# Channel attention over a 384 x 384 x 384 image: eight packed blocks in place of seven, a halved second test step, and a second pass that opens in places of 18 rows

## The chip, the cores and the metric

One NeuronCore of a Trainium2 chip. The metric is the device time of one execution in microseconds, as the median of the runs given. x has 113 MB, the core's on-chip memory (SBUF) holds a quarter of it, so x must be read, for the most part, twice.

## The reference

```python
xf = x.reshape(B, H * W, C)                    # bfloat16, 147456 x 384
gap, gmp = jnp.mean(xf, 1), jnp.amax(xf, 1)    # sum and maximum of each channel
h_a = gap @ w1; h_a = h_a * (h_a > 0)
h_m = gmp @ w1; h_m = h_m * (h_m > 0)
scale = sigmoid(h_a @ w2 + h_m @ w2)
return x * scale[:, None, None, :]
```

A first pass over x makes one sum and one maximum for each of 384 channels; a tiny network turns them into 384 scales; a second pass multiplies x by them. The scales need the whole of x.

## The kernel before

**Rows.** x is cut into 1152 *rows*: a row here is 384 channels on each of 128 partitions, 128 x 768 B = 98,304 B. The tensor `rows` holds 280 *body* rows and 5 *held* rows; `acc` holds 11 more. What stays on chip from the first pass is only multiplied and written in the second; all else is read again.

**First pass** (the loop over `steps`; each load is issued at L373 on SyncE's queue SP). For each load, TensorE adds up the channels (`sums`, L276: a matmul with a vector of ones, three at a time for a group of up to four rows), VectorE takes maxima into `acc` (L342). Loads go round through the same body places: a load waits until VectorE, TensorE and, where a packed block is in the way, ScalarE have done with what lies there. Not more than eight transfers are under way, since each semaphore is used again by the eighth after it.

**Packed blocks.** Seven blocks of 32 rows are kept in 24 rows each: `homes` holds three parts of 8 rows, `fourth` the fourth part. ScalarE first tests the block (`test`): L303 squares a scaled high byte and stores a byte, L304 squares that byte less 4 and sums it up, five pairs for a block; a sum that isn't zero means that some value does not fit the packed form, and then the blocks are read again at the end. `pack(i, half)` does half a block: TensorE makes words out of the high bytes (L324, 24 matmuls into the PSUM tile `words`), ScalarE moves low bytes into the freed places (L330, two copies) and stores the words (L331). After that the place of the fourth part is free. `judge` (L337 to L339) adds the tests up; L555 and L556 read the verdict.

**Between the passes.** `turn_sums` (L286 and L287) turns the sums by copies on ScalarE and matmuls on TensorE, `tail_sums` (L292) takes the last four loads, and `turn_over` (L348) lays a block of eight rows aside in the PSUM tile of `words`. The weights are loaded (L402, L403), a block of eight rows is loaded into the place that `turn_over` freed (`refill`, L415), `acc` is folded to one row and its rows are loaded again (L413). L404 to L407 are the mean's half of the network, L426 to L431 the maximum's half, L432 and L433 make `scale_bc`.

**Second pass.** VectorE multiplies (L438), writes are issued from ScalarE's queue (L447, L453, L492), reads from SP's (L531). First come the rows that stayed: `OPENING`, acc, the held rows, the two blocks of eight, then the 96 rows of the ring. As each place of the ring is written, a block of x is read into it (`read`), in `PLACES` of 24 and later 30 rows; the ring is body rows 0 to 96, and 0 to 120 once packed block 1 is finished. One *turn* multiplies a place, issues its write and the next read, and then does that turn's `jobs`: `unpack(i, half)` (L470 and L475 on VectorE, six copies of L489 on ScalarE) or `finish(i)`, which multiplies the block's 24 + 8 rows. Blocks 0 and 1 are written by `finish(1)`, the others beside the last three turns (`after`).

Every engine works through its own list in program order, as written out by hand; a wait of one instruction holds up all that stand behind it on its engine or queue.

Of the kernel before, what the change touches and what calls it, by code (L numbers as in the profile page):

```python
# [8 lines left out]
ACT = mybir.ActivationFunctionType  # L9
# [4 lines left out]
F32 = mybir.dt.float32  # L14
# [15 lines left out]

RING = 96
G = 8
PACKED = 7

HOME_AT = (96, 184, 128, 152, 256, 232, 208)
D_AT = (120, 176)
BODY_ROWS = 280
FIRST_AT = (0, 104, 40, 64, 200, 176, 152)  # L40
FOURTH_AT = (24, 96, 32, 88, 128, 136, 144)

TOGETHER = (1, 2, 3)
SLOTS = ((0, 31), (31, 31), (62, 34))
SPARE = 93
PSUM_ROWS = 8
LATE_ROWS = 8
BANK_ROWS = 2
RING_BYTES = 256
HELD_ROWS = 5  # L50
# [26 lines left out]
FIRST_READ = (8, 16)  # L77
FILLS = 13
# [11 lines left out]
def kernel(  # L90
# [31 lines left out]
    def take(n):  # L122
        nonlocal at
        at += n
        return at - n, n
# [4 lines left out]
    late_block, kept_block, held_block = (take(sum(pieces)) for pieces in LAST_HELD)  # L130
    stay = [take(n) for _, n in SLOTS]
    refill = take(LATE_ROWS)
    passing_at, n_pass = at, TOT - at
    between = [[take(n) for _, n in group] for group in BETWEEN]
    passing = [take(n) for _, n in PASSING]
    last_passing = take(sum(LAST_PASSING[1]))
    assert at == TOT and sum(n for _, n in PLACES) == n_pass and held_block[1] == HELD_ROWS
    assert late_block[1] == LATE_ROWS and kept_block[1] == G and [sum(p) for p in STAYING] == [n for _, n in SLOTS]
    at = passing_at
# [27 lines left out]
    held, body = rows[:, 0:HELD_ROWS, :], rows[:, HELD_ROWS:HELD_ROWS + BODY_ROWS, :]  # L167
    slots = [body[:, lo:lo + n, :] for lo, n in SLOTS]
    spare = body[:, SPARE, :]
    homes = [body[:, lo:lo + 3 * G, :] for lo in HOME_AT]  # L170
    d_places = [body[:, lo:lo + G, :] for lo in D_AT]
    fourth = [d_places[i % 2] for i in range(PACKED)]
    tested = held[:, 0:G // 2, :].rearrange("p n c -> p (n c)").bitcast(U8)
    tests = held[:, G // 2, :].bitcast(F32)
    test_bias = tests[:, NT:NT + 1]
    minus4 = tests[:, NT + 1:NT + 2]
    test_sum = tests[:, NT + 2:NT + 3]
    test_copy = tests[:, NT + 3:2 * NT + 3]

# [28 lines left out]
    nc.vector.memset(test_bias, 4.5 * TEST_SCALE)  # L208
    nc.vector.memset(minus4, -4.0)
    make_identity(nc, ident_bf)  # L210
# [21 lines left out]
    def fill(block, lo):  # L232
        load(block, body[:, lo:lo + block[1], :], (block[1],))

    for i in range(PACKED):
        if i in TOGETHER:
            lo = min(HOME_AT[i], D_AT[i % 2])
            load(packed_block, body[:, lo:lo + GP, :], (GP,), min(FIRST_AT[i], FOURTH_AT[i]))
        else:
            load(packed_block, homes[i], (FIRST_LOAD, 3 * G - FIRST_LOAD) if i == 0 else (3 * G,), FIRST_AT[i])  # L240
            load(packed_block, fourth[i], (G,), FOURTH_AT[i])
        steps += [("test", i, 0), ("pack", i, 0), ("test", i, 1), ("test", i, 2)]
        if i == 0:
            fill(first_block, 0)
        for k, b in enumerate(between[i]):
            fill(b, BETWEEN[i][k][0])
            if k == PACK_BEHIND[i]:
                steps.append(("pack", i, 1))
    for k, b in enumerate(passing):
        fill(b, PASSING[k][0])  # L250
    fill(refill, REFILL_AT)
    load(last_passing, body[:, LAST_PASSING[0]:, :], LAST_PASSING[1])
    for k, pieces in enumerate(STAYING):
        load(stay[k], slots[k], pieces)
        if k == 0:
            steps.append(("judge",))
    for block, buf, pieces in zip((late_block, kept_block, held_block), (*d_places, held), LAST_HELD):
# [39 lines left out]
    def test_one(rows, k):  # L297

        run = rows.shape[1] if len(rows.shape) == 2 else rows.shape[1] * rows.shape[2]
        out_ = tested[:, 0:run]  # L300
        if len(rows.shape) == 3:
            out_ = out_.rearrange("p (r n) -> p r n", r=rows.shape[1])
        nc.scalar.activation(out=out_, in_=rows, func=ACT.Square, bias=test_bias, scale=TEST_SCALE)  # L303
        nc.scalar.activation(  # L304
            out=out_, in_=out_, func=ACT.Square, bias=minus4, accum_out=tests[:, k:k + 1],
        )
# [29 lines left out]
    def judge():  # L336
        nc.scalar.activation(out=test_copy, in_=tests[:, 0:NT], func=ACT.Copy, accum_out=test_sum)  # L337
        nc.scalar.copy(out=total, in_=test_sum)
        nc.tensor.matmul(bad_ps, lhsT=total, rhs=ones_bf, start=True, stop=True)  # L339

# [21 lines left out]
    for st in steps:  # L362
# [51 lines left out]

    nc.sync.dma_start(out=d_places[0], in_=rows_of(xr, refill))  # L415
    load_acc(folds[-1], A)
# [37 lines left out]


    turns = len(PLACES)
    homes_d = [d_places[i % 2] for i in range(4)]
    homes_d += [homes[1][:, G * i:G * (i + 1), :] for i in range(3)]
    assert len(homes_d) == PACKED
    HG = G // 2  # L460
# [36 lines left out]
    def finish(i):  # L497

        for rows in (homes[i], homes_d[i]):
            multiply(rows, rows)  # L500
        if i == 1:
            store_packed(HOME_AT[0], GP, 0)
            store_packed(D_AT[1], GP, FOURTH_AT[1])


    jobs = [[(unpack, 0, 0)], [(unpack, 0, 1)], [(unpack, 1, 0)], [(finish, 0)], [(unpack, 1, 1)], [], [(finish, 1)]]
    jobs += [[], [], [], [(unpack, 2, 0)], [(unpack, 2, 1)]]
    for i in range(3, PACKED):
        jobs += [[(unpack, i, 0)], [(finish, i - 1)], [(unpack, i, 1)]]
    jobs.append([])  # L510
    jobs.append([(finish, PACKED - 1)])

    after = [(D_AT[0], 2 * GP, FOURTH_AT[2]), (HOME_AT[5], 6 * G, FIRST_AT[5]), (HOME_AT[1], 6 * G, FOURTH_AT[4])]

# [21 lines left out]

    def put_slot(i, lo, pieces):
        put(stay[i], slots[i][:, lo:, :], pieces, lo)

    put_slot(*OPENING)  # L540
    put_acc()
    put(held_block, held, (HELD_ROWS,))
    put(kept_block, d_places[1], (G,))
    put(refill, d_places[0], (LATE_ROWS,))
    for pieces in FIRST_PLACE:
        put_slot(*pieces)
    read(-1, 0)
    for pieces in SECOND_PLACE:
        put_slot(*pieces)
    read(-1, 0)  # L550
    for pieces in OTHER_PLACES:
        put_slot(*pieces)
    read(-1, 0)
    read(-1, 0)
    nc.vector.tensor_scalar(out=flag, in0=bad_ps, scalar1=0.5, scalar2=None, op0=ALU.is_gt)  # L555
    bad = nc.values_load(flag, engines=(ENG.SP, ENG.Activation, ENG.DVE))  # L556
    assert len(jobs) <= turns - 3
    gone = 0
# [4 lines left out]
    for turn in range(turns):  # L563
        b, buf = order.pop(0)
        multiply(buf, buf)
        if turn >= turns - len(after):
            store_packed(*after[turn - turns])
        store(buf, b, 0)
        while read(turn, gone):
            pass  # L570
        for job, *which in jobs.pop(0) if jobs else ():
            job(*which)
            gone = gone or (job is finish and which[0] == 1)
        if turn == turns - 3:
            to = leaving[1][0]
            nc.vector.tensor_copy(out=to.bitcast(U32), in_=late.bitcast(U32))  # L576
            turn_over(late, to)
            multiply(leaving[0][0][:, 0:PSUM_ROWS, :], kept_ps)
            multiply(leaving[0][0][:, PSUM_ROWS:, :], kept_b)
            multiply(to, late)  # L580
    assert not again and not order and not jobs
    for to, block in leaving:
# [38 lines left out]
```

## Time and profile before

| | us |
|---|---|
| runs shown | 724.15, 724.43 (median), 724.96 |
| the profiled execution | 724.86 |
| its span, first to last instruction | 723.1 |
| VectorE busy | 563.9 (78%) |
| ScalarE busy | 349.8 (48%) |
| TensorE busy | 183.8 (25%) |
| DMA: 192.14 MB read, 113.25 MB written | mean 423 GB/s |
| the chain that ended last: DMA, VectorE | 63%, 28% of the span |

The first pass lasts to about 270 us, the second from about 275 us to the end. Busy time is a sum over stages: ScalarE, for one, is busy for over 95% of 20 to 240 us and idle for long stretches later. A row of the table of groups gives line, engine, operation, tiles and shape, the count, busy time, mean duration in ns, and what ended the engine's idle time ahead of these instructions.

### The profile page before, as it was taken

What the parts mean: (1) busy time and instruction counts of PE and PEld (TensorE: products, weight loads), DVE (VectorE), ACT (ScalarE), POOL (GpSimd) and SP (SyncE); (2) the same over time, 40 slices, a digit from 0 to 9 for tenths busy, and PEclk for the clock granted to TensorE, in tenths of its full rate; (3) what the DMA queues carried; (4) which work ended last, traced back from release to release, by engine and by line L of the source; (5) the groups of instructions that cost most, each with busy time, mean ns of one, the idle gap of its engine ahead of it and who ended that gap; (6) DMA issues with size and microseconds to landing.
All of it is one profiled execution on the core that took longest, in us unless ns stands there. A gap on an engine that the chain in (4) does not pass through costs nothing.

```text
span 723.1 us, 3872 instructions
## 1 busy us (share of the span) xinstructions
PE 183.8 (25%) x1354; PEld 73.1 (10%) x1354; DVE 563.9 (78%) x441; ACT 349.8 (48%) x251; POOL 0.7 (0%) x6
## 2 busy tenths in 40 slices
PE   5577475966777560000000000000000000001000
PEld 1222122322222140000000000000000000001000
DVE  5698999999999998797966454798888889496200
ACT  6999999997999200057230032806244451300000
POOL 0000000000000000000000000000000000000000
PEclk9888878896978555555555555555555555555555
DMA  9999999999999979999999999999999999999997
GB/s 381 431 441 436 420 435 429 432 426 433 430 427 425 424 314 385 396 433 429 432 432 429 436 426 432 424 435 433 430 435 436 430 432 430 435 435 431 441 426 341
DMA packets 21123, 305.63 MB, mean 423 GB/s; under 512 B 2704, under 2 KB 2928, under 8 KB 8176
## 3 DMA queue, kind: packets, MB, share of 16 engines
q1 hardware_dynamic: 13760, 192.14, 62.4%
q10 hardware_dynamic: 7344, 113.25, 36.7%
q8 instruction: 10, 0.16, 0.1%
q14 instruction: 9, 0.07, 0.0%
HBM read 192.14 MB, written 113.25 MB: 422 GB/s over the span
## 4 chain that ended last, share of the span: by engine, by line
DMA 63%; DVE 28%; issue 3%; SPq 0%; DVEq 0%
DMA rows<-in_x_dram 44%; DVE acc L342 19%; DMA out_dram<-rows 18%; DVE rows L438 8%; DMA acc<-in_x_dram 1%; DVE rows L470 1%; DVE acc L438 0%; SPq L373 0%; DVE acc L475 0%; DVE acc L470 0%; SPq L531 0%; DVEq L438 0%; DVEq L342 0%
## 5 line engine op out<-in xcount | busy, mean ns | idle before, releaser
L438 DVE TENSOR_TENSOR rows<-rows,scale_bc 128x9216 bf16<-128x9216 bf16 (+9 forms) x56 | 230.9, 4166 | 93.7 <-DMA rows<-in_x_dram 92.7
L342 DVE TENSOR_TENSOR acc<-acc,rows 128x2304 bf16<-128x2304 bf16 (+4 forms) x234 | 245.2, 1126 | 12.7 <-DMA rows<-in_x_dram 12.5
L489 ACT COPY rows<-rows 128x1536 uint8<-128x1536 uint8 x28 | 41.3, 1476 | 206.4 <-DVE rows L438 205.7
L276 PE MATMUL bank_a<-rows,small 128*1 128x512 bf16 (+3 forms) x888 | 94.8, 473 | 82.0 <-DMA rows<-in_x_dram 82.0
L348 PE MATMUL words_ps<-ident_bf,acc 128*128 128x128 bf16 x24 | 2.7, 313 | 378.4 <-DVE acc L576 378.4
L303 ACT ACTIVATE rows<-rows 128x3072 uint8<-128x3072 int8 (+1 forms) x35 | 81.9, 2341 | 10.5 <-DMA rows<-in_x_dram 9.8
L304 ACT ACTIVATE rows<-rows 128x3072 uint8<-128x3072 uint8 (+1 forms) x35 | 82.0, 2344 | 1.1
L489 ACT COPY rows<-acc 128x1536 uint8<-128x1536 uint8 x42 | 60.5, 1473 | 18.2 <-DVE acc L475 17.7
L276 PEld LDWEIGHTS <-small 128*1 128x1 bf16 x888 | 30.4, 95 | 142.9 <-issue 122.0
L348 PEld LDWEIGHTS <-acc 128*128 128x128 bf16 x24 | 2.5, 148 | 378.6 <-DVE acc L576 378.6
L330 ACT COPY rows<-rows 128x1536 uint8<-128x1536 uint8 x28 | 39.7, 1468 | 0.3 <-PE words_ps L324 0.3
L324 PE MATMUL words_ps<-rows,scale_bc 128*128 128x512 fp8e4 (+1 forms) x126 | 37.0, 405 | 9.0 <-ACT rows L331 9.0
L324 PE MATMUL words_ps<-rows 128*128 128x512 fp8e3 (+1 forms) x126 | 35.1, 388 | 0.0
L470 DVE TENSOR_SCALAR rows<-rows 128x1536 uint16<-128x1536 uint16 x56 | 31.3, 560 | 1.9
L324 PE MATMUL words_ps<-rows,w_sb 128*128 128x512 fp8e3 x84 | 26.4, 398 | 0.0
L489 ACT COPY acc<-rows 128x1536 uint8<-128x1536 uint8 x14 | 20.5, 1467 | 0.0
L331 ACT ACTIVATE rows<-words_ps 128x1536 uint16<-128x1536 f32 x14 | 20.1, 1438 | 0.0
L324 PEld LDWEIGHTS <-scale_bc 128*128 128x128 bf16 x126 | 12.0, 101 | 29.2 <-issue 17.7
L324 PEld LDWEIGHTS <-rows 128*128 128x128 bf16 x126 | 12.7, 101 | 16.2 <-issue 2.4
L475 DVE SCALAR_TENSOR_TENSOR rows<-rows 128x768 uint32<-128x768 uint32 x14 | 13.4, 959 | 0.5
L475 DVE SCALAR_TENSOR_TENSOR acc<-acc,rows 128x768 uint32<-128x768 uint32 x14 | 13.4, 958 | 0.5
L286 ACT COPY w_sb<-bank_a 65x128 f32<-65x128 f32 x2 | 0.5, 261 | 25.0 <-PE bank_a L276 24.4
(61 smaller groups left out, 70.4 us busy)
## 6 DMA issues: line engine op xcount, KB each, us to landing
rows<-in_x_dram SPq DMA_DIRECT2D x16, 2880.0 KB, 26.8
out_dram<-rows ACTq DMA_DIRECT2D x15, 2880.0 KB, 21.4
rows<-in_x_dram SPq DMA_DIRECT2D x15, 2304.0 KB, 18.5
out_dram<-rows ACTq DMA_DIRECT2D x14, 2304.0 KB, 21.1
rows<-in_x_dram SPq DMA_DIRECT2D x4, 3072.0 KB, 32.1
rows<-in_x_dram SPq DMA_DIRECT2D x14, 768.0 KB, 14.0
out_dram<-rows ACTq DMA_DIRECT2D x2, 4608.0 KB, 45.6
rows<-in_x_dram SPq DMA_DIRECT2D x4, 2016.0 KB, 25.7
```

The source lines that it names most:

```text
L276: nc.tensor.matmul(sum_ps[q * QP:q * QP + 1, 0:g * P], lhsT=ones_bf[:, 0:1], rhs=rows[:, k:k + g, q * P:(q + 1) * P], start=(done + k == 0 ...
L303: nc.scalar.activation(out=out_, in_=rows, func=ACT.Square, bias=test_bias, scale=TEST_SCALE)
L304: nc.scalar.activation(out=out_, in_=out_, func=ACT.Square, bias=minus4, accum_out=tests[:, k:k + 1],)
L324: nc.tensor.matmul(words[:, c:c + BANK], lhsT=weights[2 * r + k], rhs=high(part(i, r), dt)[:, half * n + c:half * n + c + BANK], start=(r ...
L330: nc.scalar.copy(out=high(part(i, r), U8)[:, span], in_=low(part(i, r + 2), U8)[:, span])
L331: nc.scalar.activation(out=part(i, 2).rearrange("p n c -> p (n c)").bitcast(U16)[:, span], in_=words, func=ACT.Copy, bias=32767.5,)
L342: nc.vector.tensor_tensor(out=out_, in0=in0, in1=in1, op=ALU.max)
L348: nc.tensor.transpose(out=out_[:, r, q * P:(q + 1) * P], in_=rows[:, r, q * P:(q + 1) * P], identity=ident_bf)
L438: nc.vector.tensor_tensor(out=dst, in0=src, in1=scale_bc.unsqueeze(1).to_broadcast([P, n, C]), op=ALU.mult)
L470: nc.vector.tensor_scalar(out=u16(dst), in0=u16(src), scalar1=s1, scalar2=s2, op0=op0, op1=op1)
L475: nc.vector.scalar_tensor_tensor(out=u32(v), in0=u32(v), scalar=0x3F3F3F3F, in1=u32(m), op0=ALU.bitwise_xor, op1=ALU.bitwise_xor)
L489: nc.scalar.copy(out=dst, in_=src)
```

## The change

- Eight packed blocks. The eighth is loaded behind the others' (`LAST_BLOCK`, 10 and 22 rows, into body rows 64 to 96) and tested and judged there; its two pack halves are put ahead of the 19th and the 11th load from the end (`PACK_LAST`), and `judged`, the matmul of the verdict, ahead of the second half. It stays in body rows 72 to 96; rows 64 to 72 get a second block of eight rows between the passes, by a DMA ahead of the weights' loads.
- The rows that stay are body rows 0 to 64, not 0 to 96, and the loads of the first pass that only pass through at its end use these 64 rows too.
- The second step of a test reads and writes its bytes as uint16 pairs: half the elements, and the square of the pair less 0x0404.
- The second pass: a ring of 72 rows in places of 18 for twelve turns, then of 24 four times, then of 30. The eighth block's first half is unpacked ahead of the first turn. Blocks 7, 0, 2 and 3 are written when finished (`LEAVE`), the others beside the last three turns (`AFTER`); `TURNS` lists each turn's jobs (`7b` unpacks the second half of block 7, `f7` finishes it).
- `tests` has a tile of its own; the DMA scratch is 128 B, not 256.

```diff
-RING = 96
+RING = 72
-PACKED = 7
+PACKED = 8
-HOME_AT = (96, 184, 128, 152, 256, 232, 208)
-D_AT = (120, 176)
+HOME_AT = (96, 184, 128, 152, 256, 232, 208, 72)
+D_AT = (120, 176, 120, 176, 120, 176, 120, 64)
+D_THEN_AT = (120, 144, 120, 176, 136, 128, 120, 176)
-SLOTS = ((0, 31), (31, 31), (62, 34))
+STAY_ROWS = 64
-RING_BYTES = 256
+RING_BYTES = 128
-PASSING = ((62, 21), (0, 15), (15, 12), (31, 16), (47, 14))
-REFILL_AT = 62
-LAST_PASSING = (70, (6, 11))
-STAYING = ((8, 12, 11), (8, 7, 8, 8), (10, 4, 8, 4, 8))
+LAST_BLOCK = (10, 22)
+PACK_LAST = {19: 0, 11: 1}
+PASSING = ((0, 20), (20, 16), (36, 17), (53, 11), (0, 11), (11, 8), (19, 8), (27, 12))
+REFILLS = (5, 6)
+STAYING = ((39, (4, 8, 5, 8)), (0, (8, 4, 9, 8, 6, 4)))
-    ((0, 24), (24, 24), (48, 24), (72, 24)) * 3 + ((96, 24),)
-    + ((0, 30), (30, 30), (60, 30), (90, 30)) * 3 + ((0, 30), (30, 30), (60, 30), (90, 20))
+    ((0, 18), (18, 18), (36, 18), (54, 18)) * 3 + ((0, 24), (24, 24), (48, 24), (72, 24))
+    + ((0, 30), (30, 30), (60, 30), (90, 30)) * 3 + ((0, 30), (30, 30), (60, 30), (90, 12))
-FIRST_READ = (8, 16)
+FIRST_READ = (6, 12)
-OPENING = (0, 24, (3, 4))
-FIRST_PLACE = ((0, 8, (8, 8)), (0, 0, (8,)))
-SECOND_PLACE = ((1, 0, (8, 9)), (2, 0, (10,)))
-OTHER_PLACES = ((1, 17, (14,)), (2, 10, (24,)))
+OPENING = (57, (3, 4))
+FIRST_PLACE = (0, (9, 9))
+SECOND_PLACE = (18, (9, 9))
+THIRD_PLACE = (36, (18,))
+FOURTH_PLACE = (54, (3,))
+EARLY = "7a"
+TURNS = (
+    "", "7b", "", "f7", "0a", "", "0b", "f0", "", "2a", "", "2b", "f2", "3a", "3b", "f3", "", "1a", "1b",
+    "f1 4a", "4b", "f4 5a", "5b", "f5 6a", "6b", "f6",
+)
+LEAVE = {7: ((72, 24, 8), (176, 8, 0)), 0: ((96, 32, 32),), 2: ((120, 32, 64),), 3: ((152, 32, 96),)}
+GROW = (7, 0)
+AFTER = ((120, 32, 128), (184, 48, 160), (232, 48, 208))
...
+    i = PACKED - 1
+    load(packed_block, body[:, D_AT[i]:, :], LAST_BLOCK, FOURTH_AT[i])
+    steps += [("test", i, 0), ("test", i, 1), ("test", i, 2), ("judge",)]
...
         out_ = tested[:, 0:run]
+        pairs = out_.bitcast(U16)
...
         nc.scalar.activation(
-            out=out_, in_=out_, func=ACT.Square, bias=minus4, accum_out=tests[:, k:k + 1],
+            out=pairs, in_=pairs, func=ACT.Square, bias=minus, accum_out=tests[:, k:k + 1],
         )
...
+    def judged():
         nc.tensor.matmul(bad_ps, lhsT=total, rhs=ones_bf, start=True, stop=True)
...
+        if len(loads) - nth in PACK_LAST:
+            half = PACK_LAST[len(loads) - nth]
+            if half == 1:
+                judged()
+            pack(PACKED - 1, half)
         nc.sync.dma_start(out=rows, in_=rows_of(xr, block)[:, lo:hi, :])
...
+    nc.sync.dma_start(out=fourth[PACKED - 1], in_=rows_of(xr, refills[1]))
     nc.sync.dma_start(out=w1_sb, in_=w1.rearrange("(q p) m -> p q m", p=P))
...
+    put(refills[1], fourth[PACKED - 1], (G,))
     read(-1, 0)
+    work(EARLY)
...
-        for job, *which in jobs.pop(0) if jobs else ():
-            job(*which)
-            gone = gone or (job is finish and which[0] == 1)
+        if turn < len(TURNS):
+            work(TURNS[turn])
+            gone += sum("f%d" % i in TURNS[turn].split() for i in GROW)
```

More of the change, by code (lines that the diff above doesn't have):

```diff
@@ L248 @@
                 steps.append(("pack", i, 1))
+    i = PACKED - 1
+    load(packed_block, body[:, D_AT[i]:, :], LAST_BLOCK, FOURTH_AT[i])
+    steps += [("test", i, 0), ("test", i, 1), ("test", i, 2), ("judge",)]
     for k, b in enumerate(passing):
         fill(b, PASSING[k][0])
[L251 to L256, printed above, removed]
+    for lo, pieces in STAYING:
+        load(stay, body[:, lo:, :], pieces, lo)
     for block, buf, pieces in zip((late_block, kept_block, held_block), (*d_places, held), LAST_HELD):
@@ L413, in load_acc @@
         nc.sync.dma_start(out=acc[:, lo:hi, :], in_=acc_rows(xr, lo, hi))
[L415 removed]
+    nc.sync.dma_start(out=d_places[0], in_=rows_of(xr, refills[0]))
     load_acc(folds[-1], A)
@@ L500, in finish, with work @@
             multiply(rows, rows)
[L501 to L513, printed above, removed]
+        for leaves in LEAVE.get(i, ()):
+            store_packed(*leaves)
+    def work(turn):
+        for job in turn.split():
+            if job[0] == "f":
+                finish(int(job[1]))
+            else:
+                unpack(int(job[0]), "ab".index(job[1]))
     order = []
@@ L565 @@
         multiply(buf, buf)
-        if turn >= turns - len(after):
-            store_packed(*after[turn - turns])
+        if turn >= turns - len(AFTER):
+            store_packed(*AFTER[turn - turns])
         store(buf, b, 0)
@@ L580 @@
             multiply(to, late)
-    assert not again and not order and not jobs
+    assert not again and not order
     for to, block in leaving:
```

61 lines of the change are left out of this document (27 added, 34 removed).

## The prediction, made before the changed kernel was run

> **What bounds the kernel now.** First the page's slices of time and its bytes: is anything full all the time?
>
> ```profile
> DMA  9999999999999979999999999999999999999997
> GB/s 381 431 441 436 420 435 429 432 426 433 430 427 425 424 314 385 396 433 429 432 432 429 436 426 432 424 435 433 430 435 436 430 432 430 435 435 431 441 426 341
> HBM read 192.14 MB, written 113.25 MB: 422 GB/s over the span
> ```
>
> The DMA engines are busy from end to end; each slice (18.1 us) moves about 430 GB/s, except the first, the last, and the three from 253 to 307 us, where the first pass turns into the second. So time is bytes over 430 GB/s plus what that gap wastes. A row of all partitions (128 x 768 B = 98,304 B) costs 0.2286 us. I cut the gap into windows of 4 us (columns: time, busy us and count of PE, PEld, DVE, ACT, POOL, granted clock, DMA share, GB/s):
>
> ```profile
> 260.00:264.00 4.00, 1.92 (x15) 0.40 (x14) 4.00 (x6) 0.00 (x0) 0.00 (x0) 0.50 1.01 417
> 264.00:268.00 4.00, 3.64 (x45) 3.04 (x39) 4.00 (x5) 0.95 (x4) 0.00 (x0) 0.50 0.64 243
> 268.00:272.00 4.00, 3.37 (x62) 3.24 (x60) 3.90 (x7) 0.34 (x2) 0.00 (x0) 0.67 0.33 73
> 272.00:276.00 4.00, 1.04 (x7) 0.51 (x7) 2.29 (x6) 0.49 (x1) 0.00 (x0) 0.76 0.97 362
> 276.00:280.00 4.00, 0.00 (x0) 0.00 (x0) 3.83 (x5) 0.00 (x0) 0.00 (x0) 0.50 0.94 367
> 280.00:284.00 4.00, 0.00 (x0) 0.00 (x0) 4.00 (x4) 0.00 (x0) 0.00 (x0) 0.50 0.98 403
> ```
>
> Against 430 the last five lack 187 + 357 + 68 + 63 + 27 = 702 GB/s, times 4 us / 430 = 6.5 us of idle DMA. What ends the gap stands in the timeline (start, duration):
>
> ```profile
> 240.00 0.19 ACT L338 CAST small<-rows 128x1 bf16<-128x1 f32 x1
> 264.64 0.26 ACT L286 COPY w_sb<-bank_a 65x128 f32<-65x128 f32 x1 [24.44 <-PE bank_a L276]
> 267.40 2.72 PE L348 MATMUL words_ps<-ident_bf,rows 128*128 128x128 bf16 x24
> 271.16 0.17 ACT L404 ACTIVATE small<-bank_b 128x3 bf16<-128x3 f32 x1 [4.89 <-PE bank_b L292]
> 272.33 0.28 PE L426 MATMUL bank_a<-ident_bf,acc 128*128 128x128 bf16 x2 [0.69 <-DVE acc L342]
> ```
>
> Two chains meet: VectorE's maxima end in L426 at 272.33; the sums on TensorE and ScalarE (L286, L404) are through 0.7 us earlier (PE idle 0.69 before L426). ScalarE, busy from 20 to 240 us, then waits 24.4 us for L286. That idle time is the room of the change. Last, the prices by shape:
>
> ```profile
> L304 ACT ACTIVATE rows<-rows 128x3072 uint8<-128x3072 uint8 x21 | 60.0, 2856 | 0.7
> L303 ACT ACTIVATE rows<-rows 128x3072 uint8<-128x3072 int8 x21 | 59.9, 2851 | 10.0 <-DMA rows<-in_x_dram 9.8
> L330 ACT COPY rows<-rows 128x1536 uint8<-128x1536 uint8 x28 | 39.7, 1468 | 0.3 <-PE words_ps L324 0.3
> L304 ACT ACTIVATE rows<-rows 128x1536 uint8<-128x1536 uint8 x14 | 22.1, 1575 | 0.5
> L331 ACT ACTIVATE rows<-words_ps 128x1536 uint16<-128x1536 f32 x14 | 20.1, 1438 | 0.0
> ```
>
> **The bytes.** None is saved: rows read twice are 782 + 8 + 11 before (second-pass places, refill, acc) and 774 + 8 + 8 + 11 now, 801 both times. Eight of them move from the second pass, which is full, to the new refill DMA behind the first pass, into the 6.5 us of idle DMA: 8 x 0.2286 = 1.83 us gained. The cover is that gap; without it the gain is 0.
>
> **The test's second step** (L304) now has half the elements. No row shows an ACTIVATE from and to uint16; bounds: no gain (2.856 us) and 1.44 (L331, which writes uint16). I take the row of the same operation and count, 1.575; for 768 elements 1.575 - 768 x (2.856 - 1.575)/1536 = 0.935. A block saves 3 x 1.281 + 2 x 0.640 = 5.12 us of ScalarE.
>
> **The eighth block on ScalarE**, the step on which most hangs, since its pack stands in program order ahead of L286's copies. Before, a block takes 32.2 us without waits (207.55 to 239.76 in the timeline); now 32.2 - 5.1 = 27.1. Block 5 starts at 175.43 as before (ScalarE waits for its load there) and ends near 202.9 with 0.4 us of waiting for TensorE's words. Block 6 can't start before its load lands (TensorE starts on it at 203.81): 203.85. Its first pack half waits some 1.4 us for TensorE, whose 24 products start only behind the sums of 32 rows: end at 203.85 + 27.1 + 1.4 = 232.3. Block 7's 32 rows land at about 224, so no wait: tests 27.1 - 2 x 4.1 = 18.9 to 251.1, judge 0.5, first pack half 4.1: 255.7. Only then is PSUM free for TensorE's last 24 products. The like case, block 6's second half after a wait of 2.8 us, took 220.82 to 228.84 = 8.0 us with a granted clock of 0.53, then 0.96; bounds 5.4 (178.76 to 184.1, all at full clock) and 10.2 (24 x 0.427, the spacing at half clock). With 8.0: 263.8; ScalarE's two copies and words end 2.9 us later, 266.7. Behind these products in TensorE's queue stand the sums of seven loads (47 rows), 13 groups of 0.21 us at full clock (48 matmuls in 3.41 us at 228.77): 266.8. So L286 starts at 266.8 instead of 264.64, 2.2 us late. TensorE, though, comes out of a dense stretch, and the clock stayed at 1.00 through 229 to 236 after the like stretch; at full clock the 24 transposes (2.72 us) and the 39 and 24 short products (1.20, 0.78) halve, 2.1 us less. With the 0.7 us of slack, L426 is 0 to 1.5 us late; I take 0.2.
>
> The Trainium skill (TensorE: Matmul & The Clock Gate, What's actually happening) says the gate watches a free-running window of 3413 ns, so how many products run at half rate depends on the phase: by it the last pack would take an estimated 6.9 to 8.6 us. The row's 8.0 lies inside, so the sum would stand; its phase is why I keep both ends.
>
> **First pass otherwise.** VectorE has 238 maxima before and after; by shape their sum is the same 265.8 us (0.150 us + 0.52 ns per element, from the rows of 768 to 2304 elements). It is busy from 185 us on, so it ends at 270.3 again unless a load comes late. The passing loads now have 64 rows, not 96; the tightest, the one into rows 0 to 11, waits for the maxima of rows 0 to 20, done near 233, and is wanted by the DMA near 239. Waits: 0.1 us.
>
> **Second pass.** A turn of 18 rows gives the DMA 36 x 0.2286 = 8.2 us, VectorE 3.75 (24 rows take 4.96), with half an unpack 5.3 more (311.30 to 316.68), with a finish 6.7 (4.96 + 1.75). Turns 0 to 15 with the early half: VectorE 12 x 3.75 + 4 x 4.96 + 8 x 5.3 + 4 x 6.7 = 134 us, DMA 752 rows = 172. The heaviest stretch, turns 17 to 25: 9 x 6.16 + 8 x 5.3 + 4 x 6.7 = 125 against 123, with 90 other rows of the ring in flight. A ring of 72 holds 54 rows beside the place on VectorE: reading and writing these is 24.7 us of DMA, while its worst turn is 10.5 us. So no idle DMA: 0. Four more multiplies and 17.7 us of unpack copies are hidden by the same slack. At the end 32 rows fewer are left for the writes-only stretch (677 to 721 us, about 427 GB/s in its middle against 432): 0.1 us gained.
>
> **Sum**, on the profiled run's 724.86 us (span 723.1, 1.8 around it): - 1.83 + 0.2 + 0.1 - 0.1 = -1.6 us. That run is 0.4 above the median of 724.43; applied to the median: **722.8 us**, its own range 721.8 to 724.2.
>
> **Rivals.** (1) *The last pack sets the end of the first pass*, the other side. It decides once L286 starts later than about 268.5 (2.2 late is free, by the 2.1 and 0.7 above; 1.83 more eats the gain). All at half clock: products end 266.0, 13 groups x 0.427 to 271.6, L286 7 us late, L426 6.3 late, 724.4 + 6.3 - 1.8 = 729. If byte pairs save only half of the 5.1 us, blocks 6 and 7 end 4 us later: 727. Should they save nothing, L286 starts near 279: 736. For: products, words and sums follow one another with no slack. Against: the clock rose within 5.5 us in the like stretch. (2) *The ring of 72 starves the DMA* in turns 0 to 11: a read waits for its place's write to land. For: a place's own cycle is 8.2 us of DMA, some 10 on VectorE, up to 5 on ScalarE ahead of the write, about 2.3 of latency on each side (the refill of 8 rows, issued at 270.16, feeds work only after 272): 28 of the 33 us a lap has. Against: 5 us over. Price: 2 us in each of 3 laps = 6: 728.8. (3) *The refill misses the gap*: issued at 266.7 behind the last pack, it pushes the weights' loads and those of acc behind it and these set the start of the second pass: gain gone, 724.4. For: all share SP's queue. Against: 1.83 us fit into 268 to 272, where 73 GB/s move. (4) *More is gained*: the start of the reads (343 and 374 GB/s from 292 to 300) loses less with smaller places: 1.3 us more, 721.5.
>
> The Trainium skill (DMA: Bandwidth & Descriptors, Anatomy of one DMA) gives each transfer a constant of about 2.0 us beside its bytes; were it not overlapped, the six extra transfers of the smaller places would cost an estimated 12 us, 735. Loads of 8 rows at 417 to 426 GB/s (244 to 264 us) speak against it; it is part of rival 2.
>
> **How the numbers follow.** Forecast 56 in 100, rivals 1: 17, 2: 8, 3: 13, 4: 6. A difference under 0.2% (1.45 us) can't be told from no change: the forecast's 1.6 is just beyond it, so its 56 split into 43 faster and 13 same. Rival 1: 14 slower, 3 same; 2: 5 and 3; 3: 12 same, 1 slower; 4: faster. Faster 0.49, same 0.31, slower 0.20. From 721.5 to 726.8 leaves out the dear half of rival 1 and most of 2.
>
> **What would show it.** ScalarE's second step at 1.58 and 0.94 us; the last pack's words before 268 us and the first copy of the sums (L300 now) by 267.5; first multiply at 274.8 to 275.5; 264 to 272 us with 8 rows more moved; no slice under 425 GB/s after 310 us. I am wrong if L300 comes after 268.5, or if slices of the early second pass fall below 425.

## The result, and the profile after

| kernel | median of its executions, us | lowest to highest | against before on the same chip |
|---|---|---|---|
| before | 724.99 (20) | 724.15 to 726.38 | |
| changed | 727.39 (20) | 724.71 to 729.24 | 1.0026, 95% interval 1.0017 to 1.0036 |

The change costs 2.4 us where 1.6 us of gain were forecast. The profiled execution of the changed kernel took 724.8 us (span 723.0), one of its best, so it shows only a part of the loss: where 2 us of the first pass went. First the page's slices, as before of 18.1 us each:

```profile
DMA  9999999999999999999999999999999999999997
GB/s 381 435 434 433 421 432 429 428 427 430 428 421 428 414 382 347 406 424 429 430 429 431 433 434 435 429 437 433 430 428 432 433 438 428 428 432 433 450 424 334
```

The DMA engines are still busy from end to end. But slices 3 to 14 sum to 5125, against 5158 in the kernel before: 33 x 18.1 us / 430 = 1.4 us lost over the first pass. Then the windows of 4 us at the change of passes (same columns as in the prediction):

```profile
260.00:264.00 4.00, 4.00 (x16) 1.67 (x15) 3.89 (x6) 0.54 (x1) 0.00 (x0) 0.79 1.01 406
264.00:268.00 4.00, 3.50 (x45) 1.30 (x43) 3.87 (x6) 3.97 (x5) 0.00 (x0) 1.00 0.94 352
268.00:272.00 4.00, 3.87 (x95) 3.79 (x95) 4.00 (x6) 0.48 (x2) 0.00 (x0) 1.00 0.74 264
272.00:276.00 4.00, 1.47 (x15) 0.76 (x11) 2.77 (x7) 0.34 (x2) 0.00 (x0) 0.92 0.95 313
276.00:280.00 4.00, 0.14 (x1) 0.00 (x0) 3.25 (x4) 0.49 (x1) 0.00 (x0) 0.50 0.81 309
280.00:284.00 4.00, 0.00 (x0) 0.00 (x0) 4.00 (x4) 0.00 (x0) 0.00 (x0) 0.50 0.97 393
```

The gap has filled much as forecast: 264 GB/s where 73 moved, and by the prediction's count over the last five windows 519 GB/s are lacking, 4.8 us of idle DMA for 6.5. And the last pack's chain, in the timeline (start, duration, idle time before and what ended it):

```profile
252.81 0.20 ACT L354 CAST small<-tests 128x1 bf16<-128x1 f32 x1
255.66 1.44 ACT L347 ACTIVATE rows<-words_ps 128x1536 uint16<-128x1536 f32 x1
257.15 1.44 PE L340 MATMUL words_ps<-rows,scale_bc 128*128 128x512 fp8e4 x3 [2.11 <-ACT rows L347]
264.65 2.71 PE L290 MATMUL bank_a<-rows,small 128*1 128x512 bf16 x39
266.22 1.44 ACT L347 ACTIVATE rows<-words_ps 128x1536 uint16<-128x1536 f32 x1
267.56 0.25 ACT L300 COPY w_sb<-bank_a 65x128 f32<-65x128 f32 x1
272.15 1.94 DVE L360 TENSOR_TENSOR acc<-acc 128x1536 bf16<-128x1536 bf16 x3
274.15 0.28 PE L450 MATMUL bank_a<-ident_bf,acc 128*128 128x128 bf16 x2 [1.14 <-DVE acc L360]
276.75 1.63 DVE L462 TENSOR_TENSOR rows<-rows,scale_bc 128x1152 bf16<-128x1152 bf16 x2 [1.17 <-ACT scale_bc L457]
```

Of the kernel before, the two lines to compare the last three with:

```profile
270.33 1.95 DVE L342 TENSOR_TENSOR acc<-acc 128x1536 bf16<-128x1536 bf16 x3
274.76 1.63 DVE L438 TENSOR_TENSOR rows<-rows,scale_bc 128x1152 bf16<-128x1152 bf16 x2 [1.00 <-ACT scale_bc L433]
```

Read from the end. The first multiply is at 276.75 against 274.76 before: 2.0 us late. It hangs on L450 (L426 before), and TensorE stood idle 1.14 us before that for VectorE's maxima. So the late engine is VectorE (last folds at 272.15, before 270.33), not the pack's chain, which the prediction feared most. VectorE was fed late: the trace's semaphore updates put the landing of load 24 at 176.21 us against 175.41 before, of the last load at 270.41 against 268.45. Loads 0 to 24 are the same in both kernels. So the first pass runs slower well before the new block. From the first multiply on, this execution takes 723.0 - 276.75 = 446.25 us against 448.34, 2.1 us less: in this execution the rows moved out of the second pass are gained there. The loss of 2.0 and this gain cancel, which is why this execution equals the one profiled before (724.86). What makes the median 2.6 us longer is not in this profile.

ScalarE's steps by shape (busy us, mean ns):

```profile
L320 ACT ACTIVATE rows<-rows,tests 128x1536 uint16<-128x1536 uint16 x24 | 37.8, 1576 | 0.8
L320 ACT ACTIVATE rows<-rows,tests 128x768 uint16<-128x768 uint16 x16 | 15.0, 935 | 0.5
```

### The profile page after: what moved, and what is told of

Same layout as the page of the kernel before. It is cut to its first block, busy times and chain, and to the rows that moved or that the text cites. A ratio compares the mean times of both kernels' runs of the same rounds, so it can differ in the third digit from the quotient of the medians.

```text
span 723.0 us, 4062 instructions
## 1 busy us (share of the span) xinstructions
PE 191.6 (26%) x1405; PEld 75.5 (10%) x1405; DVE 574.5 (79%) x463; ACT 358.8 (50%) x284; POOL 0.7 (0%) x6
## 4 chain that ended last, share of the span: by engine, by line
DMA 53%; DVE 25%; issue 6%; ACT 5%; PE 4%; SPq 0%; DVEq 0%; ACTq 0%
DMA rows<-in_x_dram 41%; DVE rows L462 14%; DMA out_dram<-rows 11%; DVE acc L360 5%; DVE rows L490 3%; ACT rows L319 3%; PE bank_a L290 2%; PE words_ps L340 2%; ACT rows L320 1%; DVE acc L495 1%; DVE acc L490 1%; ACT rows L346 1%; ACT rows L347 0%; DVE acc L462 0%; SPq L396 0%
## 5 line engine op out<-in xcount | busy, mean ns | idle before, releaser
L462 DVE TENSOR_TENSOR rows<-rows,scale_bc 128x11520 bf16<-128x11520 bf16 (+8 forms) x60 | 231.6, 3897 | 79.0 <-DMA rows<-in_x_dram 66.7
L509 ACT COPY rows<-rows 128x1536 uint8<-128x1536 uint8 x32 | 47.2, 1476 | 155.7 <-DVE rows L462 126.4
L290 PE MATMUL bank_a<-rows,small 128*1 128x512 bf16 (+2 forms) x891 | 92.4, 466 | 80.4 <-DMA rows<-in_x_dram 80.3
L319 ACT ACTIVATE rows<-rows,tests 128x3072 uint8<-128x3072 int8 (+1 forms) x40 | 93.6, 2341 | 21.9 <-DMA rows<-in_x_dram 21.1
L509 ACT COPY rows<-acc 128x1536 uint8<-128x1536 uint8 x48 | 69.1, 1473 | 39.1 <-DVE acc L495 38.6
L346 ACT COPY rows<-rows 128x1536 uint8<-128x1536 uint8 x32 | 45.5, 1471 | 23.9 <-PE words_ps L340 23.9
L320 ACT ACTIVATE rows<-rows,tests 128x1536 uint16<-128x1536 uint16 (+1 forms) x40 | 52.8, 1319 | 1.3
L340 PE MATMUL words_ps<-rows,scale_bc 128*128 128x512 fp8e4 x144 | 43.7, 417 | 3.8 <-ACT rows L347 3.8
L340 PE MATMUL words_ps<-rows 128*128 128x512 fp8e3 x144 | 39.6, 385 | 0.0
L490 DVE TENSOR_SCALAR rows<-rows 128x1536 uint16<-128x1536 uint16 x64 | 35.8, 560 | 2.2
L340 PEld LDWEIGHTS <-w_sb 128*128 128x128 bf16 x96 | 10.0, 104 | 13.5 <-issue 3.8
```

What stands on the lines that cost most here:

```text
L290: nc.tensor.matmul(sum_ps[q * QP:q * QP + 1, 0:g * P], lhsT=ones_bf[:, 0:1], rhs=rows[:, k:k + g, q * P:(q + 1) * P], start=(done + k == 0 ...
L320: nc.scalar.activation(out=pairs, in_=pairs, func=ACT.Square, bias=minus, accum_out=tests[:, k:k + 1],)
L340: nc.tensor.matmul(words[:, c:c + BANK], lhsT=weights[2 * r + k], rhs=high(part(i, r), dt)[:, half * n + c:half * n + c + BANK], start=(r ...
L346: nc.scalar.copy(out=high(part(i, r), U8)[:, span], in_=low(part(i, r + 2), U8)[:, span])
L462: nc.vector.tensor_tensor(out=dst, in0=src, in1=scale_bc.unsqueeze(1).to_broadcast([P, n, C]), op=ALU.mult)
L490: nc.vector.tensor_scalar(out=u16(dst), in0=u16(src), scalar1=s1, scalar2=s2, op0=op0, op1=op1)
```

## The experiments

All ratios are against the kernel before on the same chip; they go by all executions, so they can differ from that of the medians.

**The last pack, the byte pairs, the place of the rows.** The diff has one line that the prediction put at nothing: `RING_BYTES` falls from 256 to 128. That moves `rows`, held rows and body, from byte 256 of each partition to byte 128.

The changed kernel again:

> The changed kernel once more, for the trace of another run: its 20 times lie between 724.7 and 729.2 us with most near 727.5, and the profile shown is of a run at 724.8. If the last pack half sets the end of the first pass in most runs (theory 1), a run near 727.5 shows the first copy of the sums (L300) after 269 us, not 267.6 as in the profile shown, VectorE's folds done before it, and the first multiply of the second pass near 279 instead of 276.75. If the ring of 72 rows starves the DMA (theory 2), the first multiply stays near 277 and slices after 300 us fall below 425 GB/s. If the first pass is only fed more slowly (theory 3), the maxima end late, near 275, with L300 well before them.

725.44 us (724.82 to 728.29), ratio 1.0018 (1.0007 to 1.0028), first multiply at 276.85. The profiled execution was again one of the best (724.82), so no profile shows a run near 727.5 of this kernel; the third, further down, is of 724.81.

The three tests of block 7 are left out, so that its pack starts earlier:

```
-    NT = 5 * PACKED
+    NT = 5 * (PACKED - 1)
...
-    steps += [("test", i, 0), ("test", i, 1), ("test", i, 2), ("judge",)]
+    steps += [("judge",)]
```

> The changed kernel without the three test pairs of block 7, some 18.9 us of ScalarE ahead of the last pack; block 7 is then not tested. Theory 1 (last pack late): the last pack half no longer waits for ScalarE, L300 comes near 265.8 us, and the time falls by 2.5 us or more to 722 to 724, below the kernel before. Theories 2 and 3 (ring; slower feeding): no change from the changed kernel, 726.5 to 728.

726.99 us (724.85 to 728.77), ratio 1.0025 (1.0014 to 1.0035); first multiply at 276.91. Nothing gained: the last pack isn't the cause.

This profile is of the longest execution, 728.77 us. Its first multiply is only 0.2 us behind that of the changed kernel's profile, and its span is 4.0 us longer (727.0 against 723.0): what sets this long execution apart lies in the second pass. One stretch of it, in the changed kernel at 724.8 and then here (DMA share and GB/s last):

```profile
460.00:480.00 20.00, 0.00 (x0) 0.00 (x0) 12.14 (x4) 1.25 (x1) 0.00 (x0) 0.50 1.01 434
```

```profile
460.00:480.00 20.00, 0.00 (x0) 0.00 (x0) 11.37 (x4) 3.80 (x3) 0.00 (x0) 0.50 1.00 408
```

That is 1.2 us; more goes at the end, where two of the 16 DMA engines finish behind the others (below).

The byte pairs alone, in the kernel before:

```
-    nc.vector.memset(minus4, -4.0)
+    nc.vector.memset(minus4, -float(0x0404))
...
+        pairs = out_.bitcast(U16)
...
-            out=out_, in_=out_, func=ACT.Square, bias=minus4, accum_out=tests[:, k:k + 1],
+            out=pairs, in_=pairs, func=ACT.Square, bias=minus4, accum_out=tests[:, k:k + 1],
```

> The kernel before with the test's second step on byte pairs, nothing else. ScalarE is done with block 6 near 232 instead of 239.8 us, which nothing waits for. All theories: within 0.5 us of the kernel before; a second step that disturbs the transfers (theory 3b) would make it 1 us or more slower.

724.81 us, ratio 0.9998 (0.9990 to 1.0007): harmless.

The rows' start alone, in the kernel before:

```
-RING_BYTES = 256
+RING_BYTES = 128
```

> The kernel before with the body rows 128 B lower (the DMA scratch 128 B instead of 256), nothing else. In the changed kernel's profile loads 0 to 24, which are the same in both, land 0.8 us later at 176 us. If the new offset slows the transfers (theory 3a), the time rises by 2 to 3 us, 726.5 to 728. If not (theory 1 or 2), it stays within 0.5 us of the kernel before.

727.53 us (726.24 to 728.78), ratio 1.0033 (1.0021 to 1.0045). One number costs 2.5 us. The profile is of the longest execution, 728.78 us, but what follows lies in the first pass. The traffic between 10 and 260 us, of the kernel before and then of this one (DMA view: packets, bytes, mean rate):

```profile
DMA packets 7100, 107.55 MB, mean 430 GB/s; under 512 B 784, under 2 KB 784, under 8 KB 2617
```

```profile
DMA packets 6935, 106.87 MB, mean 427 GB/s; under 512 B 766, under 2 KB 766, under 8 KB 2453
```

In the same 250 us 0.68 MB less come in, 1.6 us at 430 GB/s. The first multiply follows:

```profile
277.08 1.62 DVE L438 TENSOR_TENSOR rows<-rows,scale_bc 128x1152 bf16<-128x1152 bf16 x2 [1.17 <-ACT scale_bc L433]
```

It is 2.3 us late, more than in the changed kernel; the 0.7 us beyond the 1.6 were not traced.

**Place or scratch?** `RING_BYTES` is also the size of the DMA scratch. Three more versions of the kernel before: a scratch of 128 B with the rows left at 256; rows at 384 (`RING_BYTES = 384`); rows at 320 (`RING_BYTES = 320`).

```
-    nc.dynamic_dma_scratch_size = RING_BYTES
-    nc.lookup_mloc("DynamicDMAScratchLoc").dims = [P, RING_BYTES]
+    nc.dynamic_dma_scratch_size = 128
+    nc.lookup_mloc("DynamicDMAScratchLoc").dims = [P, 128]
```

> The kernel before with a DMA scratch of 128 B and the body rows left at 256 B. If the place of the rows decides: no change, 724.5 to 725.5. If the size of the scratch decides: 727 to 728.

> The kernel before with body rows at 384 B (a scratch of 384 B), that is 128 B past a multiple of 256 as in before_ring128. If the place within 256 B decides: 2 to 3 us slower than the kernel before, 727 to 728. If a small scratch or an address below 256 decided: no change from 725.

> The kernel before with its rows starting at 320 B, 64 past a multiple of 256 (scratch 320 B). Theory M (what counts is whether the start is a multiple of 256 B: an unaligned transfer of a partition touches one piece of 256 B more, wherever in it it starts): 727.2 to 727.8, as at 128 and 384. Theory B (the cost grows with the bytes past the multiple): 726.0 to 726.6. Theory H (only 64 B alignment counts, 128 and 384 are odd for another reason): 724.8 to 725.3.

Scratch alone: 724.86 us, ratio 1.0005 (0.9994 to 1.0015). Rows at 384: 727.40, ratio 1.0033 (1.0020 to 1.0046), first multiply at 277.22. Rows at 320: 726.88, ratio 1.0027 (1.0017 to 1.0038), first multiply at 277.25. The same DMA view, 10 to 260 us, scratch alone and then rows at 320:

```profile
DMA packets 7099, 107.53 MB, mean 430 GB/s; under 512 B 785, under 2 KB 785, under 8 KB 2616
```

```profile
DMA packets 6930, 106.85 MB, mean 427 GB/s; under 512 B 765, under 2 KB 765, under 8 KB 2448
```

So what counts is whether a partition's rows start on a multiple of 256 B; 64 B past it the first pass loses what it loses 128 past it. By the whole time 320 lies between its theories' ranges, so that alone would not have decided. In the trace's DMA records a packet of 24 rows (18432 B) of the first pass takes 686 ns in the median at 256 and 689 at 128, one of 8 rows 234 and 236 (means 687.3 and 690.9, 234.5 and 237.9). The excess summed over the first pass is 1.6 us for each DMA engine: 3.6 ns on average for each of its 456 packets (57 loads, 128 partitions over 16 engines). But not every packet has it. The loads of the first 30 us have none: a packet of 30 rows at 14 to 21 us takes 855 ns at 256, 128, 320 and 384, and one of 21 rows takes 601 ns near 10 us at all four, but near 40 us 601 at 256, 606 at 128 and 384 and 604 at 320. In the second pass the packets take the same at every start (18 rows 516 ns, 24 rows 686, medians). The Trainium skill (DMA: Bandwidth & Descriptors, How a descriptor splits into AXI transactions) says that an unaligned descriptor starts at the 256 B boundary below it and pays for the bytes in front. That names the boundary, and 128 B at one engine's 26.8 GB/s would be an estimated 4.8 ns a packet, near the 3.6. But by it 64 B in front should cost half of that, and every packet should pay; the records show the same excess for both, and none early in the first pass and in the second. It also speaks of bytes fetched: in the first pass the moved rows are the end that is written, and the second pass's writes, which fetch from these rows, show no excess. So the start of the rows is shown as the cause, and how it costs time is not.

**The changed kernel with its rows at 256.** That leaves 128 B less for `tests`. It shrinks to 32 floats; ten sums and the three constants lie in the last, unused 64 B of `w1_sb`, and one small ScalarE instruction adds the ten behind block 1.

```
-RING_BYTES = 128
+RING_BYTES = 256
...
-    tests = consts.tile([P, NT + 4], F32)
+    tests = consts.tile([P, 32], F32)
+    extra = w1_sb.rearrange("p q m -> p (q m)")[:, 2 * P:2 * P + 32].bitcast(F32)
...
+            nc.scalar.activation(out=extra[:, 4:14], in_=extra[:, 4:14], func=ACT.Copy, accum_out=tests[:, 0:1])
```

> The changed kernel with its body rows at 256 B again, as in the kernel before; the room comes from keeping ten of the test sums and the three test constants in unused bytes of the w1 tile, which adds one small ScalarE sum after block 1. Theory A (the start of the rows, 256 B or 128 B, is what costs 2.5 us, and the rest of the change gains its 1.8): 722.3 to 723.3 us, ratio 0.9965 to 0.998, first multiply near 275 us. Theory B (the change itself loses, the start of the rows is a second thing): 725 us or more. Theory C (the start matters, but the last pack then sets the end of the first pass): 723.5 to 724.5, with VectorE waiting for TensorE ahead of the folds' reduction.

> The same at 256 B, without the test pairs of block 7 (block 7 is not tested), so that its last pack half comes some 5 us earlier. Theory A: the same time as after_256 within 0.3 us. Theory C: 0.7 us or more below after_256.

> The changed kernel with its rows at a multiple of 256 B, unchanged, as the comparison on this chip for the two runs beside it. All theories: median 725.5 to 726.6, single executions from 722.9 to 727.5, first multiply near 276.0.

726.22 us (722.91 to 727.49), ratio 1.0007 (0.9995 to 1.0019); on a second chip 725.89 (723.27 to 727.12), ratio 1.0007 (0.9994 to 1.0019). Without the tests of block 7: 725.56 (722.90 to 727.01), ratio 1.0006 (0.9996 to 1.0015), 0.7 us less, between what theories A and C asked for and, in this spread, not to be told from nothing. The best executions now reach the forecast, the median doesn't: it lies in the range of theory B, the change loses something of its own. The timeline of the second one, profiled at 723.27:

```profile
265.21 0.25 ACT L303 COPY w_sb<-bank_a 65x128 f32<-65x128 f32 x1
270.42 1.94 DVE L363 TENSOR_TENSOR acc<-acc 128x1536 bf16<-128x1536 bf16 x3
275.01 1.63 DVE L467 TENSOR_TENSOR rows<-rows,scale_bc 128x1152 bf16<-128x1152 bf16 x2 [1.17 <-ACT scale_bc L462]
```

With the feeding restored VectorE's folds come at 270.42 (before 270.33) and the first multiply at 275.01, within the forecast's 274.8 to 275.5, with the last pack in place. The first run's profile had 276.02, with VectorE again the last, folds at 271.43; without the tests it was 275.14. That 1 us is a late load:

```profile
237.44 10.17 DVE L363 TENSOR_TENSOR acc<-acc,rows 128x1920 bf16<-128x1920 bf16 x10 [1.05 <-DMA rows<-in_x_dram]
```

By its semaphore updates 15 DMA engines had delivered this load by 235.84 us and the 16th at 237.34; in the second run all 16 had by 235.96, and VectorE didn't wait. So no run shows that the pack costs anything.

**The second pass.** There is then a spread of 4 us between executions of one kernel; those of the kernel before lie within some 2 us, single ones apart. First the size of the places in the ring of 72, with rows at 256. The jobs are laid out anew for the number of turns, and the stores of the rows that stay are cut to fit; all else is the same:

```
-    ((0, 18), (18, 18), (36, 18), (54, 18)) * 3 + ...
+    ((0, 24), (24, 24), (48, 24)) * 3 + ...
-    "", "7b", "", "f7", "0a", "", "0b", "f0", "", "2a", "", "2b", "f2", ...
+    "", "7b", "f7", "0a", "", "0b f0", "", "2a", "2b", "f2", ...
```

and likewise six places of 12 and two of 36.

> The same, but the ring of 72 opens the second pass in six places of 12 rows instead of four of 18 (60 rows instead of 54 are in flight beside the place that VectorE has, in 18 turns instead of 12). Theory S (the ring of 72 has too little slack: a read waits for the write of its place, so a lagging DMA engine makes it run dry, which is what spreads the executions over 4 us): more rows in flight, so fewer executions above 724; median 723.3 to 724.8. Theory N (the lag comes from the chip's memory or its DMA engines, whatever the ring): same spread, median within 0.7 us of the 18-row kernel. Theory F (each transfer has a fixed cost that isn't hidden): 6 reads and 6 writes more, 0.5 to 2 us slower than with 18 rows.

> The same, but with three places of 24 rows (48 rows in flight beside the one on VectorE). Theory S: less slack, reads run dry in every lap, 728 or more. Theory N: within 0.7 us of the 18-row kernel. Theory F: 0.3 to 1 us faster.

> The changed kernel with rows at a multiple of 256 B and three places of 24 rows, a second time and on another chip. If its gain over the kernel before is real: 723.6 to 724.5, ratio under 1. If it was that chip: 725 or more.

> The same with two places of 36 rows in the ring of 72 (only 36 rows in flight beside the one that VectorE has, 16.5 us of DMA). Theory P (fewer and larger transfers keep the 16 DMA engines together): 723.5 to 724.5, spread of the updates of a transfer under 2 us. Theory S' (here the slack does run out: a place's cycle is 16.5 us of DMA, some 17 on VectorE with a finish and an unpack, and the latencies, against 33 us for a lap): reads run dry, 727 or more, and idle DMA between 300 and 360 us.

| places in the ring of 72 | median, us | lowest to highest | ratio |
|---|---|---|---|
| 12 rows | 725.90 | 724.72 to 726.82 | 1.0011 (1.0002 to 1.0020) |
| 18 rows (as changed), same chip | 725.89 | 723.27 to 727.12 | 1.0007 (0.9994 to 1.0019) |
| 24 rows, same chip | 724.04 | 723.21 to 725.74 | 0.9989 (0.9980 to 0.9998) |
| 24 rows, another chip | 724.01 | 722.45 to 727.04 | 0.9984 (0.9969 to 0.9998) |
| 36 rows | 736.23 | 735.72 to 737.85 | 1.0156 (1.0143 to 1.0169) |

Theory S, too little slack in a ring of 72, falls for 18 rows: fewer rows in flight (24-row places) are better, by 1.9 us. (The intervals of 18 and 24 rows on the one chip just overlap; the second run with 24 rows, and the first with 18, 726.22, say the same.) That 24 rows gain is the sign of theory F, though it asked for 0.3 to 1 us; but by F 12 rows should have been slower than 18, and they were not. No theory here accounts for all three. At 36 theory S' holds. The page's slices of that kernel, and its window from 330 to 340 us:

```profile
DMA  9999999999999998998999999999999999999997
GB/s 383 431 430 448 417 432 436 426 434 427 429 430 424 421 344 347 396 360 343 426 376 414 410 409 416 438 435 428 426 437 438 423 440 426 436 431 428 440 437 341
```

```profile
330.00:340.00 10.00, 0.00 (x0) 0.00 (x0) 9.74 (x9) 3.68 (x3) 0.00 (x0) 0.50 0.74 260
```

In slices 18 and 19 (313 to 350 us) 360 and 343 GB/s move, and from 330 to 340 us the DMA engines are idle for a quarter of the time: each read waits for its place's write to land, and only one other place is in flight meanwhile. (Reads wait for such writes in every one of these kernels, 96 us in sum from 300 to 420 us in the kernel before and 97 here; what differs is whether anything else is in flight.) Against it the same window and the slices with 24 rows, where slices 18 and 19 have 416 and 426:

```profile
330.00:340.00 10.00, 0.00 (x0) 0.00 (x0) 10.00 (x4) 0.00 (x0) 0.00 (x0) 0.50 0.98 418
```

```profile
GB/s 385 432 440 435 417 438 430 430 428 436 428 423 433 420 389 351 405 416 426 435 430 428 435 418 436 430 434 430 433 433 432 432 432 432 436 433 424 441 435 345
```

Then the two parts crossed: small places alone in the kernel before (ring of 96, eight places of 12 for four of 24), and places of 24 in the changed kernel as it stands, rows at 128:

```
-    ((0, 24), (24, 24), (48, 24), (72, 24)) * 3 + ((96, 24),)
+    tuple((lo, 12) for lo in range(0, 96, 12)) * 3 + ((96, 24),)
```

> The kernel before with its ring of 96 in eight places of 12 rows instead of four of 24, nothing else: 12 reads and 12 writes more, and more rows in flight. Theory P (small places alone let the DMA engines drift apart): 725.7 to 727, single executions spread over 3 us, updates of a transfer more than 3 us apart after 330 us. Theory R (the drift comes from the ring of 72 or from the packed blocks' stores, not from small places): 725.0 to 725.6, spread of the updates as in the kernel before.

> The changed kernel as it is, rows at 128 B, but with its ring of 72 in three places of 24 rows instead of four of 18. Theory P (two causes that add: the start off a multiple of 256 B, about 2.4 us, and the small places, about 1.9 us in the median by the run at 256 B): 725.5 to 726.5, with a first multiply at 276.8 as before, and its single executions within 3 us of each other. Theory O (the place within 256 B alone; the places matter only at 256 B): 727.0 to 727.6, as the changed kernel.

> The changed kernel as it is, once more, on the chip of the run beside it. 725.4 to 727.5 by its two earlier medians (725.44 and 727.39).

> The changed kernel with rows at 128 B and three places of 24 rows, a second time, now beside the changed kernel on one chip. Theory P (the places cost it time at 128 B too, as they do at 256 B): 0.8 to 2 us under the run beside it, about 725.8. Theory O (at 128 B the places change nothing, the start of the rows is the whole loss): within 0.6 us of the run beside it.

Small places alone: 726.56 us (725.56 to 731.18), ratio 1.0023 (1.0010 to 1.0036). So they cost time in the kernel before too. Places of 24 with rows at 128: 726.28 (725.40 to 733.37), ratio 1.0025 (1.0007 to 1.0043), and on the next chip 726.40, ratio 1.0020 (1.0011 to 1.0029), beside the changed kernel's 727.43, ratio 1.0034 (1.0022 to 1.0047). The difference of 1.0 us is what theory P asked for at least, but the intervals overlap, and the best executions of the changed kernel (724.81) are under the best with 24 rows (725.41). At 128 the part of the places is likely, not shown.

What do small places do? The DMA records give a packet of 12, 18, 24 and 30 rows 347, 516, 686 and 855 ns: 169 ns for each 6 rows and 8 ns on top, whatever the size. Three laps of four places, not three, are 3 reads and 3 writes more, 6 x 8 packets x 8.3 ns = 0.4 us for each engine; places of 12 in the kernel before are 12 and 12 more, 24 x 8 x 8.3 = 1.6 us, and 1.4 were measured. For 18 against 24 rows that is 0.4 of 1.9 us. By the same count 12 rows should cost 0.8 us more than 18, and the medians are alike, so this price alone decides little. In long executions something else is seen and not explained: one or two of the 16 DMA engines end behind the others. The semaphore updates of the kernel's last write, one per engine (first, 15th, 16th, in us):

```
before                    719.7  721.0  721.2
rows at 256, 18 rows      720.3  721.7  723.2   (execution of 726.71 us)
rows at 256, 24 rows      718.5  719.9  720.0   (execution of 723.35 us)
before, places of 12      720.9  722.1  726.8   (execution of 730.52 us)
changed, no last tests    720.8  723.8  725.2   (execution of 728.77 us)
```

The lag is not the whole of a long execution: with rows at 256 and 18 rows that of 726.71 us ends its 15th engine at 721.7, the one of 723.27 us at 719.6; 1.0 us of these 2.1 is there at the first multiply already, by the late load above. Also the reads that follow a stretch without reads run slower in one execution than in another of the same kernel (18 rows, at 256). Windows from 416 to 440 us, of the execution of 726.71 us and of that of 723.27 (DMA share and GB/s last):

```profile
416.00:440.00 24.00, 0.00 (x0) 0.00 (x0) 14.22 (x5) 5.33 (x4) 0.00 (x0) 0.50 1.01 415
```

```profile
416.00:440.00 24.00, 0.00 (x0) 0.00 (x0) 16.72 (x5) 3.93 (x3) 0.00 (x0) 0.50 1.01 430
```

The engines don't idle in either; in the first their packets take longer (reads of 24 rows 717.5 ns in the mean, against 695.0). Why an engine lags, and why these reads are slower, was not found.

## Why the prediction was wrong

**The step that failed: an edit costed at nothing.** The prediction speaks of bytes, engines and rings, and passes over the smaller scratch, which moves the rows to byte 128. Alone it costs 2.5 us (2.3 by the run at 384, 1.8 by that at 320), more than the whole forecast gain. In the sum the term that it broke is "Waits: 0.1 us" for the first pass, with VectorE ending "at 270.3 again unless a load comes late": loads came late, the last landed at 270.41 for 268.45, and the first multiply came at 276.75 for a forecast of 274.8 to 275.5, 2.0 us. The prediction had the row that could have warned: the kernel is bound by 430 GB/s, so whatever lengthens the packets counts.

**The second miss: "no idle DMA: 0" for the ring.** No idle DMA was right (the share stays at 1.0), zero was not. The prediction cited loads of 8 rows at 417 to 426 GB/s against a cost of 2.0 us for each transfer, and then put that cost at nothing. A part of the price stood in these rows: 6144 B in 234 ns are 26.3 GB/s, 420 over 16 engines, 2 to 3% under the large packets. (The 2.0 us, taken from the Trainium skill, DMA: Bandwidth & Descriptors, Anatomy of one DMA, stand there for the path through GpSimd. Here SyncE and ScalarE issue, and 12 reads and 12 writes more cost 1.4 us in all.) At 256 the places of 18 cost 1.9 us in the median against places of 24: 0.4 us of it by this price, the rest open.

**The sum.** Both undone, the kernel takes 724.04 and 724.01 us, 1.0 and 1.15 under the kernel before, of 1.6 forecast. With the start alone put back it takes 2.2 to 2.4 more (726.28, 726.40), with the places alone put back 1.9 more (725.89). Both together would be 728.3; measured were 727.39, 725.44 and 727.43, so they don't add up in full. That the executions of one kernel lie some 4 us apart makes each such median uncertain: the changed kernel's own differ by 2.0 from chip to chip.

**What held.** The moved rows: 2.1 us less from the first multiply on (in one of the best executions), and 264 GB/s for 73 in the gap. The test's second step: 1.576 and 0.935 us for the 1.575 and 0.935 taken. The last pack: products 257.15 to 264.65, 7.5 us for 8.0, first copy of the sums at 267.56 for 266.8, just past the 267.5 named as a sign and under the 268.5 from which it would have decided; with rows at 256 it is at 265.21 and 266.40. TensorE's clock read 1.00 from 264 to 272 us, where it had been 0.50 and 0.67, as argued.

**The rivals.** (1) The last pack sets the end: no; VectorE did, and leaving out three tests gained nothing at 128. (2) The ring of 72 starves the DMA: not with 18 rows (the slice from 307 to 325 us shows 424 for 433, one under the sign of 425, with the DMA share at 1.0), but with 36 by the mechanism described. (3) The refill misses the gap: no, 264 GB/s. (4) More gained by smaller places at the start: the windows of 292 to 300 us moved 340 and 418 GB/s for 343 and 374, some 0.4 us; places of 18 lose more in all. None of the four was the cause; the list lacked a change of address.

## What to carry to other kernels

When a kernel moves a buffer, if only because a neighbour shrank, look at the new start within 256 B before anything else: in this kernel, bound by its transfers, 3.6 ns a packet were 1.6 us of the first pass. Cost a ring's places by both bounds: too large and reads wait for writes, too small and each packet's fixed time adds up; here 24 rows were best, and 12, 18 and 36 worse. Where the executions of a kernel spread over 4 us, profile a long one too: the best ones of the changed kernel looked like the kernel before. And compare packets of different sizes in the trace: a rate a few per cent lower for small ones is a fixed cost, to be multiplied by the number that the change adds.

## What the runs showed of the hardware

- A start of a partition's rows 64 or 128 B off a multiple of 256 B lengthened the packets of the first pass, which only reads, by 3.6 ns on average (128: 686 to 689 ns in the median for 24 rows), but not in its first 30 us (855 ns for 30 rows at every start), and not those of the steady second pass, where reads and writes mix (516 ns for 18 rows at both starts). 64 B past cost as much as 128. Why is not shown.
- A packet has some 8 ns beside its bytes: 347, 516, 686, 855 ns for 9216, 13824, 18432, 23040 B.
- One of 16 DMA engines ended up to 4.7 us behind the other fifteen at a kernel's end, in some executions (before with places of 12, 730.52 us). It was seen in long executions of versions of the kernel; how much it adds to the changed kernel's own spread of 4.5 us isn't known, and its cause is open.
